# Two attention layers and two gated feed-forward layers: the last chunk's head groups reordered and packed, a norm's reciprocal deviation issued earlier

## The chip, the cores and the metric

The kernel runs on one core of a Trainium2 chip. The metric is the device time of one execution in microseconds (us), lower being better. In the text the engines are PE (TensorE matmul; PEld is its weight load), DVE (VectorE), ACT (ScalarE), POOL (GpSimd) and SP (SyncE, which here only issues DMAs).

## The reference

Four sublayers run one after the other over a residual x of 2048 positions by 448 features, all in float32; the same weights serve both passes.

```
def A(x, wq, wk, wv, wo):             # 16 query heads of 28, one key and value head
    q = (x @ wq) split in 16 heads;  k = x @ wk;  v = x @ wv
    p = softmax(q k^T * 28 ** -0.5)
    return (p @ v, heads joined) @ wo
def B(x, w_gate, w_up, w_down):       # 448 -> 1792 -> 448
    return (silu(x @ w_gate) * (x @ w_up)) @ w_down

x = x + A(layernorm(x));  x = x + B(layernorm(x))
x = x + A(layernorm(x));  x = x + B(layernorm(x))
```

## The kernel before

Positions are cut into four chunks of 512 (`c`), each of four tiles of 128. Matmuls run on float32 numbers split into a high and a low part (`split`, L138 to L140: two POOL instructions), so each product takes three matmuls: high by high, high by low, low by high.

**Scores.** `Attention.scores` works through `GR` (L367), a list of sixteen pairs (chunk, group). A group holds four heads, which sit on 32 partitions each: 28 rows of the head and four spare rows. Each group has sixteen steps (`kt`), one for every 128 keys. A step (L688) runs twelve score matmuls into four PSUM banks (four at a time on 32 rows of the array), and ACT takes the exponential of three banks at once (L704, L710) and of the fourth (L707, L709); on odd steps DVE first copies the fourth bank to SBUF (`raw`, L706). After each odd step the values of the pair of steps before are multiplied in (`pv`, L729) and DVE adds them to the group's accumulator (L746; the first of a group is a copy, L743). One column of the values is 1, so row 28 of each head holds the sum of its exponentials.

**Division.** When a group's last pair is in, `post` (L750) lets SP move the four sum rows to a tile `rs` (L757). Some steps later `rest` runs: five small DVE instructions ending in the reciprocal (L763 to L765), a DMA to DRAM (`rd`, L767), one DMA that broadcasts it to 128 partitions (`rb`, L768, destination 4 x 32 partitions x 512), a multiplication on POOL (L772) and a split into `on` (L773). `rb` and the accumulator `oraw` are halves of one tile (named `o` in the profile).

**Projection by wo.** For the first three chunks the fourth group is dissolved: `spread` (L629) moves the rows of its heads 14 and 15 into the spare rows of the other groups by fourteen small SBUF-to-SBUF DMAs, and copies what is left (two heads, 64 rows) to the upper half. `dense` (L635) then projects two tiles with nine matmuls each on all 128 rows, plus three on each half of the array, which run side by side (`side_by_side`, L353; profile line L358). It runs on PE in the second pair of steps of the next chunk's second group (`between`, L713). The weights `woh` and `wol` are loaded to match (`load_wo(.., True)`). For the last chunk `load_wo(.., False)` loads them again in group 14 without spare rows (memset L612, DMA L619, split on POOL), and `outproj` (L675) uses twelve full matmuls for each of the four tiles.

**Norm.** `norm_steps` (L234) gives the steps of the norm of a projected chunk: four statistics steps (`stat`), `scale` (two POOL instructions, L246 and L247, which make `rstd`), four pairs of `apply` (DVE, L255) and `turn` (DVE transpose, L260), and `send` (four DMAs, L269). The loop at L781 places them for chunks 0 to 2: statistics at steps 4 to 7 of groups 5, 9 and 13, `scale` at step 15, the pairs from step 0 of the next group, `send` at its step 8. In groups 11, 12 and 13, step 8, `weights` (L170) loads feed-forward weights on SP and splits them with twelve POOL instructions (`wgh`, `wgl`, `wdh`, `wdl`).

**End of the attention (L824 to L837).** The first two feed-forward units of chunk 0 (`unit`, L1134; matmuls L338) are laid around the last group's division: unit 0, then `rest` of the last group, then unit 1. Then `outproj` takes three groups for all four tiles, unit 0's second down projection (kept in `ff.left`) runs, and `outproj` takes the last group; DVE adds to the residual `xres`.

Each engine has its own queue and runs it strictly in the order in which the program issues; across engines there are only semaphores.

Of the kernel before, what the change touches and what calls it, by code (L numbers as in the profile page):

```python
# [8 lines left out]
F32 = mybir.dt.float32  # L9
# [43 lines left out]
def forward(  # L53
# [313 lines left out]
    GR = [(c, g) for c in range(NC) for g in range(NG)]  # L367

    class Attention:
# [230 lines left out]
        def scores(self, ff):  # L600
            next(switch)
            with tc.tile_pool(name=f"at{self.layer}", bufs=1, reuse_waits="tile") as wp:
# [6 lines left out]
                def load_wo(z, dense):  # L609
                    r = wpool.tile([P, 4, 2, P], F32, name="wr").rearrange("p (z k) b n -> p z (k b n)", z=2)  # L610
                    if not dense:
                        nc.gpsimd.memset(r, 0.0)  # L612
                    spare = wo[14 * DH : 16 * DH, :].rearrange("(q r) n -> r q n", r=4)
                    for j in range(4):
                        for up in (0, 64) if dense and z and j < 2 else (0,):
                            own = slice(2 * z + bool(up), 2 * z + (1 if dense and z and j > 1 else 2))
                            to = slice(bool(up), own.stop - 2 * z)
                            p0 = up + 32 * j
                            nc.sync.dma_start(r[p0 : p0 + DH, to, 0:D], wos[j][:, own, :])  # L619
                            if dense:  # L620
                                qs = slice(4 * own.start + j, 4 * own.stop - 3 + j, 4)
                                nc.sync.dma_start(r[p0 + DH : p0 + 32, to, 0:D], spare[:, qs, :])
# [6 lines left out]
                def spread(o):  # L629
                    for q in range(14):  # L630
                        p0 = 64 + 4 * q + 4 * (q > 6)
                        dma(o[32 * (q % 4) + DH : 32 * (q % 4) + 32, q // 4], o[p0 : p0 + 4, 3])
                    dma(o[64:128, 3], o[0:64, 3])

                def dense(c, ts, pos, half_first):  # L635
                    o = on[c]
                    cols = [slice(P * t, P * t + P) for t in ts]
                    terms = ((0, woh), (0, wol), (1, woh))

                    def half():  # L640
                        side_by_side(
                            *(
                                [
                                    (po[:, 0:D], (o[rs, 3, v, cs], b[rs, 3, :]), half_first and z == 0, z == 2 and not half_first)
                                    for z, (v, b) in enumerate(terms)
                                ]
                                for cs, po, rs in zip(cols, pos, HALVES)
                            )
                        )

                    def full_tiles(cs, po):
                        for g in range(3):
                            for z, (v, b) in enumerate(terms):
                                nc.tensor.matmul(  # L654
                                    po[:, 0:D], o[:, g, v, cs], b[:, g, :],
                                    start=(g + z == 0 and not half_first), stop=(g + z == 4 and half_first),
                                    skip_group_check=True,
                                )

                    def add(t, po):  # L660
                        x = xres[:, 4 * c + t, :]
                        nc.vector.tensor_tensor(x, po[:, 0:D], x, ALU.add)

                    if half_first:
                        half()
                    for t, cs, po in zip(ts, cols, pos):
                        full_tiles(cs, po)
                        if half_first:
                            add(t, po)
                    if not half_first:  # L670
                        half()
                        for t, po in zip(ts, pos):
# [706 lines left out]
```

## Time and profile before

| what | us |
|---|---|
| median of 3 runs | 1957.73 (1957.02 to 1959.05) |
| the profiled execution, its own time | 1955.75 |
| its span, first to last instruction | 1953.9 |
| PE busy | 1940.9 (99%) |
| ACT busy | 1340.4 (69%) |
| DVE busy | 1020.0 (52%) |
| POOL busy | 790.2 (40%) |

Times in the profile are counted from the start of the span. A row of the timeline holds start, duration, engine, line, operation, output<-inputs, shapes and how many instructions are merged in it; in brackets stands the idle time of the engine just before it, and what ended that. Matmuls overlap, so on PE the distance between starts is what one costs. Layer 0's first accumulate copy (L743) stands at 67.90 us and its last burst ends at 587.72; layer 1's at 1035.80 and 1556.11.

### The profile page before, as it was taken

The numbers are of one execution on the slowest core, as the hardware profiler recorded it, in microseconds if no ns is written. First come the engines' busy times: TensorE is split into PE (matmuls) and PEld (weight loads), VectorE is DVE, ScalarE is ACT, GpSimd is POOL, SyncE is SP. The second block draws the span as 40 slices with busy tenths as digits, with TensorE's granted clock in tenths as the row PEclk, the third lists the DMA queues.
The fourth block names the chain that finished last, engine by engine and source line by source line (L and its number), as shares of the span: only waits on it lengthen the run. The fifth ranks groups of instructions, "written<-read, shape, count | busy, mean of one in ns | idle before, by whom it ended". The sixth has DMA issues, their size and how long they took to land. (4 is left out here: it accounts for less than half of the span.)

```text
span 1953.9 us, 45906 instructions
## 1 busy us (share of the span) xinstructions
PE 1940.9 (99%) x18307; PEld 1303.6 (67%) x18307; DVE 1020.0 (52%) x1711; ACT 1340.4 (69%) x2353; POOL 790.2 (40%) x1021
## 2 busy tenths in 40 slices
PE   9999999999999999999999999999999999999998
PEld 8544444545458889999984445444444688999997
DVE  7443454544435567665654334445545345666653
ACT  4899899898963344444349998989989533444442
POOL 5222111132414868766441221111334167688640
PEclk9999999999999999999999999999999999999999
DMA  5110120021310110010131111202122101110002
GB/s 167 54 32 24 31 56 25 19 76 39 87 35 2 53 33 21 28 32 27 53 114 32 29 29 27 63 23 55 37 64 64 33 11 44 33 32 22 28 17 77
DMA packets 102555, 84.49 MB, mean 43 GB/s; under 512 B 26832, under 2 KB 84816, under 8 KB 102336
## 3 DMA queue, kind: packets, MB, share of 16 engines
q1 hardware_dynamic: 101760, 80.60, 14.8%
q8 instruction: 144, 2.36, 0.5%
q10 hardware_dynamic: 576, 0.92, 0.1%
q14 instruction: 75, 0.61, 0.1%
HBM read 58.99 MB, written 18.74 MB: 40 GB/s over the span
## 5 line engine op out<-in xcount | busy, mean ns | idle before, releaser
L736 PE MATMUL bank<-pt,vsb 128*32 128x512 f32 x4096 | 493.3, 598 | 0.3
L697 PE MATMUL bank<-qstack,keys 32*128 32x512 f32 x1536 | 484.0, 425 | 2.3 <-DVE raw L706 1.4
L697 PE MATMUL three<-qstack,keys 32*128 32x512 f32 x4608 | 461.2, 424 | 1.5 <-DVE vt L573 1.2
L697 PEld LDWEIGHTS three<-qstack,keys 32*128 32x128 f32 x4608 | 254.0, 182 | 294.4 <-ACT pt L710 173.5
L704 ACT ACTIVATE pt<-three 128x1536 f32<-128x1536 f32 x256 | 372.5, 1455 | 1.7 <-PE bank L736 1.3
L710 ACT ACTIVATE pt<-three 128x1536 f32<-128x1536 f32 x256 | 372.1, 1454 | 0.0
L358 PE MATMUL bank<-xh,wgh 64*128 64x512 f32 x1344 | 360.6, 392 | 0.3 <-DVE sg L1176 0.3
L358 PE MATMUL bank<-wdh,h 64*128 64x448 f32 x1776 | 326.5, 364 | 0.1
L706 DVE COPY raw<-bank 128x512 f32<-128x512 f32 x256 | 176.7, 690 | 230.6 <-PE bank L697 227.7
L358 PE MATMUL bank<-xh,wgl 64*128 64x512 f32 x1020 | 289.4, 390 | 0.0
L772 POOL TENSOR_TENSOR o<-o 128x512 f32<-128x512 f32 x32 | 41.2, 1287 | 595.2 <-DMA o<-rd 521.8
L746 DVE TENSOR_TENSOR o<-bank,o 128x512 f32<-128x512 f32 x224 | 154.8, 691 | 230.1 <-PE bank L736 222.6
L736 PEld LDWEIGHTS bank<-pt,vsb 128*32 128x32 f32 x4096 | 107.1, 109 | 250.2 <-issue 153.7
L365 ACT COPY seen<-bank 128x1 f32<-128x1 f32 x788 | 101.0, 164 | 242.9 <-PE bank L358 182.3
L358 PE MATMUL bank<-xl,wgh 64*128 64x512 f32 x912 | 252.0, 390 | 0.0
L697 PEld LDWEIGHTS bank<-qstack,keys 32*128 32x128 f32 x1536 | 243.3, 183 | 4.5 <-DVE raw L706 2.0
L358 PEld LDWEIGHTS bank<-wdh,h 64*128 64x128 f32 x1776 | 233.5, 184 | 10.8 <-issue 2.0
L358 PE MATMUL bank<-wdl,h 64*128 64x448 f32 x888 | 209.7, 366 | 0.0
L358 PEld LDWEIGHTS bank<-xh,wgh 64*128 64x128 f32 x1344 | 197.2, 184 | 13.4 <-issue 1.1
L962 POOL TENSOR_TENSOR xres<-stage,xres 128x448 f32<-128x448 f32 x120 | 151.6, 1275 | 112.9 <-ACT stage L955 112.7
L927 DVE TENSOR_TENSOR xn<-bank,xn 128x512 f32<-128x512 f32 x192 | 126.6, 687 | 125.9 <-PE bank L358 91.4
L709 ACT ACTIVATE pt<-bank 128x512 f32<-128x512 f32 x256 | 151.6, 592 | 54.9 <-PE bank L697 54.8
(214 smaller groups left out, 3066.6 us busy)
## 6 DMA issues: line engine op xcount, KB each, us to landing
o<-rd SPq DMA_DIRECT2D x32, 256.0 KB
qraw<-qd SPq DMA_DIRECT2D x128, 56.0 KB
qd<-stage SPq DMA_DIRECT2D x30, 224.0 KB
xt<-xn SPq DMA_DIRECT2D x28, 224.0 KB
wdr<-in_B_w_down_dram SPq DMA_DIRECT2D x28, 224.0 KB
wr<-in_B_w_gate_dram SPq DMA_DIRECT2D x32, 192.0 KB
wr<-in_B_w_up_dram SPq DMA_DIRECT2D x32, 192.0 KB
xn<-xt SPq DMA_DIRECT2D x6, 768.0 KB
```

Source lines behind the costliest of these rows:

```text
L358: nc.tensor.matmul(po, a, b, start=start, stop=stop, skip_group_check=True)
L365: nc.scalar.copy(seen[:, i : i + 1], po[:, 0:1])
L697: nc.tensor.matmul(three[:, j, :] if j < 3 else one, k[js, kp, ks], q[js, part, :], start=(z == 0), stop=(z == 2), tile_position=(32 * j, 0),)
L704: nc.scalar.activation(pt, three, AF.Exp, scale=SCALE)
L706: nc.vector.tensor_copy(raw, one)
L709: nc.scalar.activation(pt1, one, AF.Exp, scale=SCALE)
L710: nc.scalar.activation(pt, three, AF.Exp, scale=SCALE)
L736: nc.tensor.matmul(po[32 * j : 32 * j + 32, :], vsb[:, n % NT, :], pts[n][j], start=(n == 2 * d), stop=(n > 2 * d), skip_group_check=True,)
L746: nc.vector.tensor_tensor(acc, in_turn(po), acc, ALU.add)
L772: nc.gpsimd.tensor_tensor(rb, oraw, rb, ALU.mult)
L927: plus = lambda out, po, r: tt(by_tile(out), in_turn(po), by_tile(r), ALU.add)
L962: nc.gpsimd.tensor_tensor(r, h[e, t], r, ALU.add)
```

## The change

1. `GR` takes the last chunk's groups in the order 3, 0, 1, 2.
2. For the last chunk's first group (head group 3) the upper 60 rows of the divided result `rb` (heads 14 and 15) are written to DRAM (`two`); `spread` then moves only two pieces (12 and 13) and the copy to the upper half.
3. For its other groups (`ahead`) `post` also sets `rb` to 1.0 on POOL (128x512) and lets SP bring four rows of `two` into the spare rows of each head's accumulator, each DMA behind the DMA that reads that head's sum; `rest` broadcasts to 28 rows of each head by four DMAs in place of one.
4. The second load of `wo` (group 14) is gone, with its memsets and splits; `outproj` is gone, and the last burst uses the packed form, two tiles at a time: the half-row matmuls of a pair of tiles, then two groups for each of the two. The third group of all tiles follows unit 0's second down projection as before.
5. The last group's `rest` is handed to unit 0 as pending work, which puts it behind ACT's cast of `h` and ahead of DVE's low part of `h` (L1180) rather than behind the unit.
6. In the norm steps of chunks 0 to 2 `scale` runs together with the fourth statistics step (step 7), and everything behind it comes three steps earlier (`apply` from step 13, `send` at step 5 of the next group).

The functions `dense` and `outproj` are cut into `half`, `whole` and `add`; for chunks 0 to 2 PE's order does not change by it.

POOL in group 13 of layer 0, before: `wdh`, `wdl` are the last of the weight splits, `qstack` the query split of group 15.

```order
L139 TENSOR_SCALAR wdh<-wdr 128x224
L140 TENSOR_TENSOR wdl<-wdr,wdh 128x224
L246 TENSOR_SCALAR rstd<-mv 128x4
L247 TENSOR_TENSOR rstd<-rstd,halfn 128x4
L139 TENSOR_SCALAR qstack_101<-qraw 128x512
```

The same place now, from the split of the divided group 12:

```order
L139 TENSOR_SCALAR on<-o_5606 128x512
L140 TENSOR_TENSOR on<-o_5606,on 128x512
L246 TENSOR_SCALAR rstd<-mv 128x4
L247 TENSOR_TENSOR rstd<-rstd,halfn 128x4
L139 TENSOR_SCALAR wgh<-wr 128x256
L140 TENSOR_TENSOR wgl<-wr,wgh 128x256
```

The two instructions that make `rstd` have moved from behind the twelve weight splits to ahead of them, right behind the division's.

PE at the start of layer 0's last burst, before (the first row is the end of unit 0's first down projection, `bank_7169` and `bank_7170` are the PSUM banks of tiles 0 and 1):

```order
L358 MATMUL bank_79<-wdh,h_7196 128x448
L680 MATMUL bank_7169<-woh,on 128x448
L680 MATMUL bank_7169<-wol,on 128x448
L680 MATMUL bank_7169<-woh,on 128x448 x2
L680 MATMUL bank_7169<-wol,on 128x448
L680 MATMUL bank_7169<-woh,on 128x448 x2
L680 MATMUL bank_7169<-wol,on 128x448
L680 MATMUL bank_7169<-woh,on 128x448
L680 MATMUL bank_7170<-woh,on 128x448
```

The same place now (`bank_7175` and `bank_7176` are those of tiles 0 and 1; L358 is on half the rows, L651 on all):

```order
L358 MATMUL bank_79<-wdh,h_7202 128x448
L358 MATMUL bank_7175<-woh,on 128x448
L358 MATMUL bank_7176<-woh,on 128x448
L358 MATMUL bank_7175<-wol,on 128x448
L358 MATMUL bank_7176<-wol,on 128x448
L358 MATMUL bank_7175<-woh,on 128x448
L358 MATMUL bank_7176<-woh,on 128x448
L651 MATMUL bank_7175<-woh,on 128x448
L651 MATMUL bank_7175<-wol,on 128x448
L651 MATMUL bank_7175<-woh,on 128x448 x2
L651 MATMUL bank_7175<-wol,on 128x448
L651 MATMUL bank_7175<-woh,on 128x448
```

Nine full matmuls of a tile ahead of the down projection have become three half ones, in pairs with those of the next tile, and six full ones.

SP at the end of layer 0's scores, before and then now (`o_6876` is the last group's accumulator and broadcast, `xd` the next stage's first transfer):

```order
L757 DMA rs<-o_6876 32x1x16 x4
L767 DMA rd<-rs 128x16
L768 DMA o_6876<-rd 128x1x512
L124 DMA xd_7332<-xh 64x512
L124 DMA xd_7333<-xh 64x512
```

```order
L738 DMA rs<-o_6876 32x1x16 x4
L744 DMA o_6876<-two 4x512 x4
L754 DMA rd<-rs 128x16
L757 DMA o_6876<-rd 28x512 x4
L124 DMA xd_7341<-xh 64x512
```

Four small moves stand between the sums and the reciprocal's way to DRAM, and the broadcast is four transfers.

The diff, without the parts that only cut `dense` into pieces:

```diff
-    GR = [(c, g) for c in range(NC) for g in range(NG)]
+    GR = [(c, (g + 3 * (c == NC - 1)) % NG) for c in range(NC) for g in range(NG)]
...
+                row = lambda q: 4 * q + 4 * (q > 6)
+
+                def spread(c):
+                    o = on[c]
+                    for q in range(14) if c < NC - 1 else (12, 13):
+                        dma(o[32 * (q % 4) + DH : 32 * (q % 4) + 32, q // 4], o[64 + row(q) : 68 + row(q), 3])
                     dma(o[64:128, 3], o[0:64, 3])
...
+                def half(c, t, two, start):
+                    side_by_side(
+                        *(
+                            [
+                                (po[:, 0:D], (on[c][rs, 3, v, cs], b[rs, 3, :]), start and z == 0, z == 2 and not start)
+                                for z, (v, b) in enumerate(terms)
+                            ]
+                            for po, cs, rs in zip(two, cols[t : t + 2], HALVES)
+                        )
+                    )
+
+                def whole(c, t, po, gs, start=False, stop=False):
+                    for g in gs:
+                        for z, (v, b) in enumerate(terms):
+                            nc.tensor.matmul(
+                                po[:, 0:D], on[c][:, g, v, cols[t]], b[:, g, :], start=start and g + z == 0,
+                                stop=stop and g + z == 4, skip_group_check=True,
                             )
...
+                    ahead = c == NC - 1 and g < NG - 1
+                    if ahead:
+                        nc.gpsimd.memset(rb, 1.0)
+                        for j in range(4):
+                            p0 = row(4 * g + j)
+                            nc.sync.dma_start(oraw[32 * j + DH : 32 * j + 32, :], on["two"][p0 : p0 + 4, :])
...
-                        nc.sync.dma_start(rb, rd[:, None, :].to_broadcast([4, 32, 512]))
-                        if g == 0:
+                        if ahead:
+                            for j in range(4):
+                                nc.sync.dma_start(rb[32 * j : 32 * j + DH, :], rd[j : j + 1, :].to_broadcast([DH, 512]))
+                        else:
+                            nc.sync.dma_start(rb, rd[:, None, :].to_broadcast([4, 32, 512]))
+                        if i % NG == 0:
                             on[c] = wp.tile([P, NG, 2, 512], F32R, name="on")
...
-                        if g == NG - 1 and c < NC - 1:
-                            spread(o)
-                            todo.append(c)
+                        if c == NC - 1 and g == NG - 1:
+                            on["two"] = dram.tile([60, 512], F32, name="two")
+                            nc.sync.dma_start(on["two"], rb[64:124, :])
+                        if g == NG - 1:
+                            spread(c)
+                            if c < NC - 1:
+                                todo.append(c)
...
+                    fs[3:5] = [lambda fs=fs[3:5]: [f() for f in fs]]
                     for kt, f in enumerate(fs):
-                        later[n + kt + (7 if kt > 3 else 0)] = f
+                        later[n + kt + (5 if kt > 3 else 0)] = f
...
-                    if i == 14 and kt in (2, 12):
-                        later[n + 7], later[n + 8] = load_wo(kt // 8, False)
...
+                ff.pend = [lambda: None, lambda: None, due.popitem()[1]]
                 ff.unit(0, 0, 0)
-                due.popitem()[1]()
                 ff.unit(0, 0, 1)
                 pos = [bank(LOW)[1] for _ in range(4)]
-                for gs in (range(NG - 1), range(NG - 1, NG)):
+                for gs in (range(2), range(2, 3)):
                     for t in range(4):
-                        add = outproj(NC - 1, t, pos[t], gs)
-                        if add:
-                            add()
+                        if 0 in gs and t % 2 == 0:
+                            half(NC - 1, t, pos[t : t + 2], True)
+                        whole(NC - 1, t, pos[t], gs, stop=True)
+                        if 2 in gs:
+                            add(NC - 1, t, pos[t])
                     while ff.left:
                         ff.left.pop(0)()
```

More of the change, by code (lines that the diff above doesn't have):

```diff
@@ L627, in load_wo @@
                     return [lambda: cast(0), lambda: cast(1)]
[L629 to L632, printed above, removed]
-                    dma(o[64:128, 3], o[0:64, 3])
[L635 to L647, printed above, removed]
-                            )
[L649 to L672, printed above, removed]
-                            add(t, po)
```

45 lines of the change are left out of this document (22 added, 23 removed).

## Prediction

> **What bounds the kernel now.** I read the page first, then the table by stage (windows), then the order of time on each engine where two equal stages differ.
>
> ```profile
> PE 1940.9 (99%) x18307; PEld 1303.6 (67%) x18307; DVE 1020.0 (52%) x1711; ACT 1340.4 (69%) x2353; POOL 790.2 (40%) x1021
> ```
>
> PE is busy nearly everywhere, so a saving must shorten what PE does or remove a place where it waits. A "group" below is the sixteen score steps of one entry of GR, numbered 0 to 15 in each layer. In the windows a row holds the stretch and its length, then the busy time of PE, PEld, DVE, ACT, POOL. The first three stretches run from the first accumulate copy (L743) of a group to that of the next, the last one over the burst that ends layer 0's attention.
>
> ```profile
> 215.85:254.41 38.56, 38.56 (x372) 20.13 (x375) 19.81 (x37) 29.62 (x33) 8.22 (x9) 1.00 0.06 15
> 470.78:510.44 39.66, 38.99 (x372) 20.18 (x375) 19.80 (x37) 29.92 (x33) 22.01 (x34) 1.00 0.19 53
> 1438.17:1478.84 40.67, 39.01 (x372) 20.16 (x375) 19.79 (x37) 29.95 (x33) 21.98 (x34) 1.00 0.19 52
> 564.56:587.72 23.16, 23.16 (x118) 19.13 (x118) 5.96 (x13) 3.07 (x9) 3.18 (x3) 1.00 0.23 57
> ```
>
> Group 5 (first row) and group 13 of both layers run the same instructions on PE, DVE and ACT (x372, x37, x33), a projection of the chunk before and its statistics included. Group 13 is 39.66 - 38.56 = **1.10 us** longer in layer 0 and 40.67 - 38.56 = **2.11 us** in layer 1, and PE has holes there that group 5 has not. The difference is POOL's 22 us against 8. In order of time:
>
> ```profile
> 494.96 1.29 POOL L140 TENSOR_TENSOR on<-o,on 128x512 fp32r<-128x512 f32 x1
> ...
> 503.30 0.20 POOL L246 TENSOR_SCALAR rstd<-mv 128x4 f32<-128x4 f32 x1
> 503.58 1.01 POOL L247 TENSOR_TENSOR rstd<-rstd,halfn 128x4 f32<-128x4 f32 x1
> ```
> ```profile
> 504.62 0.80 DVE L255 TENSOR_SCALAR sg<-xres,mv,rstd 128x448 f32<-128x448 f32 x1 [2.06 <-POOL rstd L247]
> 1473.01 0.81 DVE L255 TENSOR_SCALAR sg<-xres,mv,rstd 128x448 f32<-128x448 f32 x1 [3.06 <-POOL rstd L247]
> ```
>
> The norm's rstd stands on POOL behind twelve weight splits, from the division's end to 503.30. DVE waits for it 2.06 and 3.06 us, the raw copy that ACT needs is queued behind that wait, and so a wait of an idle engine becomes time. Price: 2.06 - 1.10 = 0.96 and 3.06 - 2.11 = 0.95 of the wait are absorbed, the rest is lost, one for one.
>
> The burst at the end (last row) has no hole: 23.16 us long, PE 23.16 busy. There only fewer matmuls help, and only if POOL's last group is ready when PE gets to it.
>
> **Term 1: rstd at the last statistics step.** Two POOL instructions move from behind the twelve weight splits to ahead of them; four applies and four transposes on DVE, and the four transfers of the turned chunk on SP, come three steps earlier, in groups 5, 9 and 13 of each layer. Now rstd follows the three POOL steps of the division (L772, L139, L140). In group 13 of layer 0 these ended at 494.96 + 1.29 = 496.25; rstd took 503.30 to 504.59, 1.29; so it would be ready at 497.5. The first apply then stands behind the raw copy of step 13:
>
> ```profile
> 496.31 0.69 DVE L706 COPY raw<-bank 128x512 f32<-128x512 f32 x1 [1.12 <-PE bank L697]
> 498.18 0.69 DVE L746 TENSOR_TENSOR o<-bank,o 128x512 f32<-128x512 f32 x1 [1.18 <-PE bank L736]
> 509.16 1.09 DVE L260 STREAM_TRANSPOSE xn<-sg 128x448 f32<-128x448 f32 x1
> ```
> ```profile
> 1463.38 1.28 POOL L140 TENSOR_TENSOR on<-o,on 128x512 fp32r<-128x512 f32 x1
> 1463.70 0.69 DVE L706 COPY raw<-bank 128x512 f32<-128x512 f32 x1 [1.13 <-PE bank L697]
> 369.36 1.02 POOL L247 TENSOR_TENSOR rstd<-rstd,halfn 128x4 f32<-128x4 f32 x1
> 369.09 0.69 DVE L706 COPY raw<-bank 128x512 f32<-128x512 f32 x1 [1.12 <-PE bank L697]
> ```
>
> DVE is free at 497.0, so the wait left is 0.5 us; in layer 1 rstd would be ready at 1464.66 + 1.29 = 1465.95 against 1464.39, a wait of 1.56. With 0.95 absorbed that costs nothing and 0.6: the cautious end of the term is 1.10 + 1.5 = 2.6 us. But the division itself should end sooner in group 13, since the weight loads that SP issued right behind its broadcast now queue behind the copy of the fourth group to DRAM and two small moves, which wait for POOL. Broadcasts on SP and POOL's start after them:
>
> ```profile
> 486.45 0.57 SPq L768 DMA_DIRECT2D o<-rd  x1
> 492.89 1.29 POOL L772 TENSOR_TENSOR o<-o 128x512 f32<-128x512 f32 x1 [11.19 <-DMA o<-rd]
> 546.78 0.57 SPq L768 DMA_DIRECT2D o<-rd  x1
> 551.96 1.28 POOL L772 TENSOR_TENSOR o<-o 128x512 f32<-128x512 f32 x1 [13.65 <-DMA o<-rd]
> ```
>
> 6.44 us with loads behind it, 5.18 without: 1.26 us sooner, which covers both waits but for 0.3. So I take the whole **3.2 us** (1.10 + 2.11), between 2.6 and 3.2. In groups 5 and 9 nothing is gained. There the closest case is group 9 of layer 0: rstd done at 370.38, DVE free at 369.78, 0.6 late, within what is absorbed. The parity of the steps turns: the apply (0.80 above, beside a busy POOL) now falls into the gap of 1.18 ahead of the accumulate and the transpose (1.09) into the gap of 1.12 ahead of the raw copy. Both fit, the second barely; an overrun of a few tenths is again absorbed, and the cover is the copy's own wait for PE.
>
> What else moves in group 13 costs nothing: the weight loads are issued some 8 us later (an estimate: after POOL's 495, in place of 487), and behind their splits stands the query split of group 15, which is not needed before that group starts. SP's four transfers of the turned chunk now go ahead of a division's sums and broadcast; the accumulator that these hold is needed a group later. The second load of wo, its two memsets and eight POOL casts go; they stood in groups 14 and 15, where POOL idled 13.65 us ahead of a division (551.96), so nothing is gained.
>
> **Term 2: the last burst.** Out go 48 full matmuls, in come 36 full and 12 on half the rows, which run in six pairs. PE, layer 0 (starts, merged rows):
>
> ```profile
> 575.88 0.37 PE L358 MATMUL bank<-wdh,h 64*128 64x448 f32 x2
> 576.18 0.47 PE L680 MATMUL bank<-woh,on 128*128 128x448 f32 x1
> 576.49 0.36 PE L680 MATMUL bank<-wol,on 128*128 128x448 f32 x1
> ...
> 583.37 0.37 PE L680 MATMUL bank<-woh,on 128*128 128x448 f32 x1
> ...
> 585.10 0.47 PE L680 MATMUL bank<-woh,on 128*128 128x448 f32 x1
> ```
>
> From 576.49 to 583.37 stand 34 matmuls: 0.2024 us each, and a pair takes one such slot. 48 slots become 42: 6 x 0.2024 = 1.21 us less. Against it stands each change between full and half rows: 575.88 to 576.18 to 576.49 is 0.61 for two slots, so 0.61 - 0.40 = 0.205 a change. The burst had four (half to full, to half, to full, to half), and has six now: 0.41 more. Net **0.80 us a layer, 1.6 in all**. The Trainium skill, "TensorEngine Tiling (Array Packing)", Key Properties, says that changing the tiling mode drains TensorE; that speaks against this change, and the rows agree with it (0.205 us). Without that rule the term would be 2.4.
>
> PE would reach the last group at 585.10 - 0.80 = 584.3 in layer 0 and, by the rows below, at 1552.7 in layer 1. POOL ended its part at 583.12 + 1.28 = 584.40 and at 1553.09:
>
> ```profile
> 583.12 1.28 POOL L140 TENSOR_TENSOR on<-o,on 128x512 fp32r<-128x512 f32 x1
> 1551.81 1.28 POOL L140 TENSOR_TENSOR on<-o,on 128x512 fp32r<-128x512 f32 x1
> 1553.49 0.47 PE L680 MATMUL bank<-woh,on 128*128 128x448 f32 x1
> ```
>
> So the chain to POOL decides. It starts earlier: the division now stands ahead of h's low part on DVE.
>
> ```profile
> 569.94 0.69 DVE L1176 TENSOR_TENSOR sg<-bank,sg 128x512 f32<-128x512 f32 x1 [4.59 <-PE bank L338]
> 571.98 0.17 DVE L763 TENSOR_SCALAR under<-rs 128x16 f32<-128x16 f32 x1
> 565.38 2.44 SPq L757 DMA_DIRECT2D rs<-o  x4
> 572.97 0.33 SPq L767 DMA_DIRECT2D rd<-rs  x1
> 574.37 0.59 SPq L768 DMA_DIRECT2D o<-rd  x1
> 581.05 1.28 POOL L772 TENSOR_TENSOR o<-o 128x512 f32<-128x512 f32 x1 [25.74 <-DMA o<-rd]
> 212.48 2.38 SPq L443 DMA_DIRECT2D qraw<-qd  x4
> 216.74 0.62 POOL L139 TENSOR_SCALAR qstack<-qraw 128x512 fp32r<-128x512 f32 x1 [15.46 <-DMA qraw<-qd]
> ```
>
> DVE can begin at 570.63 in place of 571.98, 1.35 us sooner. SP has four new moves between rs and rd, each waiting for its own sums: the last sums landed about 1.4 after their issue (as rd did, 572.97 to 574.37), near 568.6, and four issues of 0.59 end near 571.0, ahead of rd at 571.6. The broadcast becomes four transfers of 28 rows. The nearest row is four loads of 28x512: 4.26 us from first issue to POOL. By it POOL starts at 573.0 + 4.3 = 577.3 in place of 581.05, over 3 us ahead of PE. The other end: each costs what the one did (6.68) and the last is issued 1.77 later: 581.5, 0.4 us later than now; PE then waits 0.5 and 0.8 and the term falls to 0.3. I take 1.6. The Trainium skill, "DMA: Bandwidth & Descriptors", Rules for kernel authors, says that an outermost dimension below 16 confines a transfer to that many engines; the old broadcast has 4 outermost, the new ones 28 rows. The 4.26 against 5.18 agrees and lowers the chance of the second rival. The memsets to 1.0 and the noops ahead of the burst cost nothing: POOL idles 25.7 us there.
>
> **Sum.** The profiled execution took 1955.75 us (span 1953.9 and 1.85 around it), 1.98 under the median 1957.73. 1955.75 - 3.2 - 1.6 = 1950.95; on the median **1952.9 us**.
>
> **Rivals.**
> 1. *The wait in group 13 only moves*: weight splits that now run later, beside the applies of group 14, or the transposes in their tight gap, cost what was won. Only term 2 is left: 1957.73 - 1.6 = 1956.1. For it: the gap is 1.12 for 1.09. Against: 0.95 us is absorbed.
> 2. *PE waits for the last group*, as worked out above: 1957.73 - 3.2 - 0.3 = 1954.2. For it: today POOL is only 0.7 and 0.4 us ahead of PE. Against: the chain loses over a microsecond on DVE and gets shorter transfers.
> 3. *Slower*: the apply at step 13 waits at all six places. It stands three steps sooner than now, and rstd right behind a division that waits for a transfer. A rd that lands late does this: in group 13 of layer 1 it took 2.60 to the broadcast, against 1.40 at layer 0's end.
>
> ```profile
> 1452.40 0.36 SPq L767 DMA_DIRECT2D rd<-rs  x1
> 1455.00 0.57 SPq L768 DMA_DIRECT2D o<-rd  x1
> ```
>
>    Groups 5 and 9 are at most 0.6 late, so it decides from 0.35 us more. With 2.4 us late at each of the six places, 6 x 1.45 = 8.7 are lost and 4.8 won: 1961.6. One such rd is seen; six at once are not.
> 4. *More than counted*, if the changes between full and half rows hide behind pairs (0.8) or group 13 gains beyond group 5's length: near 1952.
>
> **Chances.** Forecast 0.55, rival 1 0.15, rival 2 0.14, rival 3 0.06, rival 4 0.10. A measurement of this kernel tells some 0.2%, 3.9 us, from no change: below 1953.8 is faster. The forecast lies only 0.9 under that bound, so I count 0.06 of its 0.55 as no change, and 0.01 of rival 1 as slower: faster 0.59, same 0.34, slower 0.07. The range reaches over rivals 1, 2 and 4 and leaves out the third: 1951.4 to 1956.4.
>
> **What would show it.** In the profile after: the wait of L255 for rstd in group 13 under 1 us, and the stretch between its L743 rows at 38.5 us in both layers (right), or above 39.3 (rival 1). The burst from the first matmul on the first chunk's gate weights to the next chunk's at 22.4 in place of 23.16, with no idle PE ahead of the last group (right); POOL's last split ending after PE arrives (rival 2). Waits of L255 over 1 us in groups 5 and 9: rival 3. Six changes of rows at other than 0.2 us would break term 2.

## The result, and the profile after

The median of ten executions fell from 1957.07 us (ten of the kernel before, 1955.55 to 1960.07) to **1952.31 us** (1951.67 to 1953.48): ratio 0.9975, 95% interval 0.9966 to 0.9985, so 4.8 us less (2.9 to 6.7). The profiled execution took 1952.91 us (span 1951.1), 2.84 less than that of before.

The page's line of engines, and the windows of the changed kernel: group 9 of layer 0, group 13 of both layers, and the two bursts (stretch and length, then the busy time of PE, PEld, DVE, ACT and POOL; the last three numbers are the granted TensorE clock, the busy share of the DMA engines and GB/s).

```profile
PE 1939.6 (99%) x18307; PEld 1298.2 (67%) x18307; DVE 1026.6 (53%) x1711; ACT 1338.5 (69%) x2353; POOL 778.4 (40%) x1007
```
```profile
343.58:382.76 39.18, 38.90 (x372) 20.23 (x375) 22.10 (x40) 29.75 (x33) 8.23 (x9) 1.00 0.06 15
471.39:509.95 38.56, 38.56 (x372) 20.13 (x375) 21.64 (x41) 29.62 (x33) 18.18 (x29) 1.00 0.24 65
1437.44:1476.23 38.79, 38.79 (x372) 20.17 (x375) 21.49 (x40) 29.71 (x33) 16.91 (x27) 1.00 0.24 65
564.10:586.53 22.43, 22.43 (x118) 17.87 (x117) 5.85 (x13) 3.06 (x9) 3.20 (x3) 1.00 0.24 59
1530.39:1552.82 22.43, 22.43 (x119) 17.89 (x118) 5.85 (x13) 3.06 (x9) 3.19 (x3) 1.00 0.23 58
```

Group 13 went from 39.66 to 38.56 us in layer 0 and from 40.67 to 38.79 in layer 1, and PE's holes there closed. Each burst is 0.73 or 0.74 us shorter. Group 9 of layer 0, 38.56 before, now has a hole, a stretch in which PE is idle.

POOL and DVE in group 13 of layer 0 (the first two rows), DVE in layer 1's, and DVE in group 9 of layer 0, in order of time:

```profile
496.01 1.01 POOL L247 TENSOR_TENSOR rstd<-rstd,halfn 128x4 f32<-128x4 f32 x1
497.58 0.51 DVE L255 TENSOR_SCALAR sg<-xres,mv,rstd 128x448 f32<-128x448 f32 x1
...
1464.73 0.51 DVE L255 TENSOR_SCALAR sg<-xres,mv,rstd 128x448 f32<-128x448 f32 x1 [1.08 <-POOL rstd L247]
...
371.25 0.51 DVE L255 TENSOR_SCALAR sg<-xres,mv,rstd 128x448 f32<-128x448 f32 x1 [1.43 <-POOL rstd L247]
371.68 0.68 DVE L727 TENSOR_TENSOR o<-bank,o 128x512 f32<-128x512 f32 x1
372.28 0.98 DVE L260 STREAM_TRANSPOSE xn<-sg 128x448 f32<-128x448 f32 x1
```

Where 2.06 us of waiting stood, DVE no longer waits; in layer 1 the wait fell from 3.06 to 1.08. In group 9 a wait of 1.43 is new; there the accumulate (L727) stands behind the waiting apply, and PE waits for its bank. The transpose now takes 0.98 us.

`rstd` stands behind the division, and the division waits for its reciprocal. In group 9 of layer 0 the kernel before had these rows on SP:

```profile
357.80 0.35 SPq L767 DMA_DIRECT2D rd<-rs  x1
360.19 0.58 SPq L768 DMA_DIRECT2D o<-rd  x1
```

That is 2.39 us from the write to the broadcast, and 2.75 now (357.83 to 360.58). From the broadcast to POOL's start it took 5.44 us and takes 5.88 now. Together that is 0.8 us later.

The end of layer 0's scores: SP's queue, POOL and PE.

```profile
572.56 1.59 SPq L757 DMA_DIRECT2D o<-rd  x4
575.82 1.29 POOL L763 TENSOR_TENSOR o<-o 128x512 f32<-128x512 f32 x1 [22.21 <-DMA o<-rd]
577.90 1.29 POOL L140 TENSOR_TENSOR on<-o,on 128x512 fp32r<-128x512 f32 x1
```
```profile
578.71 0.36 PE L651 MATMUL bank<-woh,on 128*128 128x448 f32 x1
579.00 0.47 PE L358 MATMUL bank<-woh,on 64*128 64x448 f32 x2
579.30 0.36 PE L358 MATMUL bank<-wol,on 64*128 64x448 f32 x2
...
583.86 0.47 PE L651 MATMUL bank<-woh,on 128*128 128x448 f32 x1
```

POOL is done at 579.19, 4.7 us ahead of PE's last group at 583.86 (0.7 before). A change of rows reads as 578.71 to 579.00 to 579.30: 0.59 for two slots of 0.20, so 0.19 for the change.

**What the two traces account for.** From the first accumulate copy to the end of the burst layer 0 took 519.82 us and now 518.51, layer 1 520.31 and now 518.10: 3.5 us. The other stages, whose instructions are the same, took 0.7 more in this one execution. The medians differ by 4.8.

### The profile page after: what moved, and what is told of

Its sections match the earlier page's. It is cut to its first block, busy times and chain, and to the rows that moved or that the text cites. A ratio compares the mean times of both kernels' runs of the same rounds, so it can differ in the third digit from the quotient of the medians.

```text
span 1951.1 us, 45958 instructions
## 1 busy us (share of the span) xinstructions
PE 1939.6 (99%) x18307; PEld 1298.2 (67%) x18307; DVE 1026.6 (53%) x1711; ACT 1338.5 (69%) x2353; POOL 778.4 (40%) x1007
## 5 line engine op out<-in xcount | busy, mean ns | idle before, releaser
L358 PE MATMUL bank<-xh,wgh 64*128 64x512 f32 x1344 | 357.8, 392 | 0.3 <-DVE sg L1172 0.3
L358 PE MATMUL bank<-wdh,h 64*128 64x448 f32 x1776 | 325.7, 364 | 0.1
L358 PE MATMUL bank<-xh,wgl 64*128 64x512 f32 x1020 | 287.7, 390 | 0.0
L727 DVE TENSOR_TENSOR o<-bank,o 128x512 f32<-128x512 f32 x224 | 154.9, 691 | 235.5 <-PE bank L717 227.5
L358 PE MATMUL bank<-xl,wgh 64*128 64x512 f32 x912 | 250.0, 390 | 0.0
L358 PEld LDWEIGHTS bank<-wdh,h 64*128 64x128 f32 x1776 | 228.6, 184 | 11.2 <-issue 2.0
L358 PE MATMUL bank<-wdl,h 64*128 64x448 f32 x888 | 207.9, 366 | 0.0
L358 PEld LDWEIGHTS bank<-xh,wgh 64*128 64x128 f32 x1344 | 193.3, 184 | 14.1 <-issue 1.1
```

The lines of the kernel that those rows point to most:

```text
L358: nc.tensor.matmul(po, a, b, start=start, stop=stop, skip_group_check=True)
L727: nc.vector.tensor_tensor(acc, in_turn(po), acc, ALU.add)
```

## The experiments

"Before" in each comparison is the kernel before, run on the same chip in between. The experiments ran on three chips, where the medians of the kernel before were 1956.74, 1957.09 and 1956.56, so a difference of half a microsecond between the medians of two kernels from different chips can't be told from none. Medians in us:

| run | median | range | ratio to before (95%) |
|---|---|---|---|
| norm edit alone | 1954.78 | 1952.63 to 1958.37 | 0.9990 (0.9981 to 0.9999) |
| packing without the norm edit | 1971.96 | 1971.64 to 1972.85 | 1.0075 (1.0061 to 1.0089) |
| before, weight splits later | 1953.10 | 1952.72 to 1954.31 | 0.9979 (0.9970 to 0.9988) |
| norm edit and later splits | 1954.11 | 1953.01 to 1955.80 | 0.9985 (0.9976 to 0.9994) |
| changed, rstd later at six places | 1968.70 | 1967.24 to 1969.30 | 1.0062 (1.0046 to 1.0077) |
| changed, applies two steps later | 1952.43 | 1951.71 to 1955.52 | 0.9977 (0.9968 to 0.9986) |
| changed, all halves first | 1953.76 | 1952.96 to 1955.76 | 0.9982 (0.9973 to 0.9991) |
| changed, halves joined | 1951.36 | 1950.71 to 1952.70 | 0.9973 (0.9963 to 0.9983) |
| halves joined, later splits in place of the norm edit | 1951.29 | 1950.58 to 1952.08 | 0.9973 (0.9961 to 0.9984) |

### The norm edit alone

```diff
+                    fs[3:5] = [lambda fs=fs[3:5]: [f() for f in fs]]
                     for kt, f in enumerate(fs):
-                        later[n + kt + (7 if kt > 3 else 0)] = f
+                        later[n + kt + (5 if kt > 3 else 0)] = f
```

> The kernel before with edit 6 alone (rstd at the last statistics step, everything behind it three steps earlier); groups in the old order, the second load of wo and the unpacked burst stay. Theory (the two terms add, and the first is the wait of group 13): 2.6 to 3.2 us less than before, 1953.9 to 1954.5 us; stretch of group 13 at 38.6 us in layer 0 and 38.6 to 39.2 in layer 1, since here the broadcast keeps its 6.44 us; burst still 23.16. The ten times should lie as close together as those of the changed kernel (1.8 us) and not as wide as those of before (4.5), if it is that wait which differs from one execution to the next. Rival (the wait only moves, and the packing won the 4.8): 1957 us, with waits of L255 elsewhere.

Measured 1954.78, 2.0 us less, short of the 2.6 to 3.2 expected. Group 13 of layer 0 is cured; in layer 1 a wait is left:

```profile
470.80:509.29 38.49, 38.49 (x372) 20.20 (x375) 21.86 (x41) 29.61 (x33) 22.05 (x34) 1.00 0.20 54
1437.17:1476.21 39.04, 38.88 (x372) 20.19 (x375) 21.99 (x41) 29.71 (x33) 22.30 (x34) 1.00 0.19 53
```
```profile
1453.75 0.58 SPq L768 DMA_DIRECT2D o<-rd  x1
1459.85 1.28 POOL L772 TENSOR_TENSOR o<-o 128x512 f32<-128x512 f32 x1 [11.29 <-DVE raw L706]
1464.62 0.59 DVE L255 TENSOR_SCALAR sg<-xres,mv,rstd 128x448 f32<-128x448 f32 x1 [1.24 <-POOL rstd L247]
```

The broadcast still takes 6.10 us to POOL's start, and the apply at step 13 waits 1.24. Group 9 of layer 0 has a wait of 1.03 and took 38.77 us. The theory's size holds for group 13 of layer 0; the times are not closer together than before, so that part of it failed.

### The packing without the norm edit

The changed kernel with the three lines above reversed.

> The changed kernel without edit 6: scale back at step 15, behind the weight splits. Theory (a wait for rstd is lost one for one but for 0.95 us): the splits now end near 511.4 and 1479.0 us, since their loads queue behind the copies of the fourth group; rstd would be ready near 512.7 and 1480.3, DVE asks for it at 502.6 and 1470.0, so 10.1 and 10.4 us of wait, 9.2 and 9.4 lost against 1.1 and 2.1 before. With 1.5 won in the two bursts that is 13.9 us more than before: 1971 us; group 13 near 47.8 us in both layers. Rival (the two parts are independent): 1.5 us less than before, 1955.6 us.

Measured 1971.96, 15.2 us more than before, and no other group changed. Windows of group 13 of both layers, then DVE and PE in layer 0:

```profile
470.35:519.03 48.68, 41.05 (x372) 21.04 (x375) 19.71 (x37) 29.95 (x33) 21.60 (x34) 0.89 0.19 52
1446.28:1495.61 49.33, 40.67 (x372) 20.97 (x375) 19.74 (x37) 29.93 (x33) 21.58 (x34) 0.90 0.19 52
```
```profile
511.62 0.81 DVE L255 TENSOR_SCALAR sg<-xres,mv,rstd 128x448 f32<-128x448 f32 x1 [9.47 <-POOL rstd L247]
513.08 0.79 PE L669 MATMUL bank<-qstack,keys 32*128 32x512 f32 x1 [7.63 <-DVE raw L678]
```

The theory's mechanism holds: packing pushes the weight loads behind the copies of the fourth group, the splits behind the loads, and rstd behind the splits. But 10.2 us are lost in layer 0 (48.68 - 38.5) with a wait of 9.47, so nothing was absorbed. The window's clock of 0.89 points to the reason; it is taken up below.

### Later weight splits in place of the norm edit

```diff
-                    if kt == 8 and 10 < i <= 11 + FG:
-                        ff.W[i - 11] = weights(i - 11)
+                    if kt == 8 and 10 < i < 11 + FG or (i, kt) == (14, 0):
+                        ff.W[min(i - 11, FG)] = weights(min(i - 11, FG))
```

> The kernel before, with the third set of feed-forward weights loaded and split from step 0 of group 14 rather than step 8 of group 13; nothing else changes, scale stays at step 15. Theory (the twelve weight splits ahead of rstd are the whole of group 13's excess): group 13 takes 38.6 us in both layers, 3.2 us less in all: 1953.9 us, with times as close together as in the changed kernel. Rival (the excess belongs to the division's late broadcast and its three POOL steps): group 13 still 39.7 and 40.7 us, 1957 us.

Measured 1953.10, 3.6 us less. Group 13, where scale was not touched, gives 3.3 of it:

```profile
471.04:509.56 38.52, 38.52 (x372) 20.14 (x375) 20.28 (x37) 29.61 (x33) 21.73 (x34) 1.00 0.21 54
1437.22:1475.70 38.48, 38.48 (x372) 20.15 (x375) 20.25 (x37) 29.59 (x33) 21.72 (x34) 1.00 0.21 54
```

The twelve splits are the whole excess of group 13, and the theory holds to 0.1 us in the windows: 1.10 and 2.11 forecast, 39.66 - 38.52 = 1.14 and 40.67 - 38.48 = 2.19 measured. The broadcast stayed late here, 6.10 and 6.40 us to POOL's start, so the rival is out.

### Both cures together

The two edits above on the kernel before.

> The kernel before with both the norm edit and the later weight splits (third set from step 0 of group 14). Theory (both take the same wait away, so they don't add): about 1953.1 us as with the later splits alone, group 13 at 38.5 us in both layers. The norm edit alone gave 1954.8 with times from 1952.6 to 1958.4; if the loads and splits in group 13 are what spreads them, they lie within 2 us here; if it is the early apply, they stay 4 us and more apart. Rival (two gains that add): 1951 us.

Measured 1954.11: they don't add. But the theory's 38.5 us in both layers did not come. The early apply still waits, 1.77 us in group 13 of layer 1 (39.47 us) and 1.23 in group 9 of layer 0 (38.99 us), and the times lie 2.8 us apart, between the two cases named. In group 13 the broadcast took 6.16 and 6.56 us to POOL's start, with loads still issued behind it: the query's, then the weights' of group 14. By these waits the later place of scale is the safer one when the splits are out of the way. The medians of the two kernels, 1953.10 and 1954.11, don't show it, since the intervals of their ratios overlap.

### rstd later at all six places

The two instructions run three times over (`times=3`):

```diff
...
-            nc.gpsimd.tensor_scalar(rstd, mv[:, 4 * c + m * z : 4 * c + m * z + m, 1], 1.0, EPS, ALU.mult, ALU.add)
-            nc.gpsimd.tensor_tensor(rstd, rstd, halfn[:, 0:m], ALU.pow)
+            for _ in range(times):
+                nc.gpsimd.tensor_scalar(rstd, mv[:, 4 * c + m * z : 4 * c + m * z + m, 1], 1.0, EPS, ALU.mult, ALU.add)
+                nc.gpsimd.tensor_tensor(rstd, rstd, halfn[:, 0:m], ALU.pow)
...
```

> The changed kernel with the two POOL instructions of scale run three times over for chunks 0 to 2 (the same result each time), so that rstd comes 2 x 1.29 = 2.6 us later at all six places. In the changed kernel's trace rstd is 0.0, 1.4 and -0.6 us late for DVE in groups 5, 9 and 13 of layer 0, and 0.0, 0.0 and 1.05 in layer 1. Theory (a wait is lost one for one but for some 0.83 us, as group 9's 1.43 gave 0.62 and group 13's 1.08 gave 0.24): waits of 2.6, 4.0, 2.0, 2.6, 2.6 and 3.6, lost 17.4 - 5.0 = 12.4 in place of 0.9, so 11.5 us more than the changed kernel: 1963.8 us. Rival (the earlier place leaves slack that the trace doesn't show): under 5 us more.

Measured 1968.70, 16.4 us more than the changed kernel, for 11.5 expected. Group 9 of layer 0, then groups 5 and 13 of layer 1 (the third number from the right is the granted clock), and a finer cut of the first of them, around the end of PE's hole:

```profile
345.43:388.55 43.12, 40.49 (x372) 20.53 (x375) 22.19 (x41) 29.88 (x33) 10.64 (x13) 0.96 0.06 14
1190.45:1232.59 42.14, 40.55 (x372) 20.61 (x375) 22.01 (x40) 29.91 (x33) 10.64 (x13) 0.96 0.06 15
1450.39:1491.10 40.71, 38.87 (x372) 20.17 (x375) 21.36 (x41) 29.72 (x33) 21.85 (x35) 1.00 0.23 62
```
```profile
376.00:378.00 2.00, 1.37 (x13) 0.64 (x17) 1.78 (x3) 0.00 (x0) 0.55 (x1) 0.93 0.00 0
378.00:380.00 2.00, 2.00 (x16) 0.43 (x8) 1.67 (x2) 0.60 (x1) 1.34 (x2) 0.50 0.00 0
380.00:382.00 2.00, 2.00 (x24) 0.87 (x20) 0.86 (x2) 1.37 (x2) 0.00 (x0) 0.72 0.00 0
```

DVE and PE in the same three groups (L256 is the apply here, L728 the accumulate, L670 a score matmul):

```profile
375.46 0.51 DVE L256 TENSOR_SCALAR sg<-xres,mv,rstd 128x448 f32<-128x448 f32 x1 [3.79 <-POOL rstd L248]
376.63 0.49 PE L670 MATMUL bank<-qstack,keys 32*128 32x512 f32 x1 [2.63 <-DVE o L728]
...
1219.47 0.51 DVE L256 TENSOR_SCALAR sg<-xres,mv,rstd 128x448 f32<-128x448 f32 x1 [2.74 <-POOL rstd L248]
1220.64 0.66 PE L670 MATMUL bank<-qstack,keys 32*128 32x512 f32 x1 [1.59 <-DVE o L728]
...
1479.58 0.51 DVE L256 TENSOR_SCALAR sg<-xres,mv,rstd 128x448 f32<-128x448 f32 x1 [2.98 <-POOL rstd L248]
1480.75 0.50 PE L670 MATMUL bank<-qstack,keys 32*128 32x512 f32 x1 [1.84 <-DVE o L728]
```

The clock is 1.00 in four of the six groups, and there the law holds: in the last row, 2.98 waited, 40.71 - 38.5 = 2.2 lost, 0.8 absorbed. In the two with 0.96 more is lost than was waited: 43.12 - 38.5 = 4.6 for 3.79, and 3.6 for 2.74. There the granted clock fell to 0.50 after PE's hole, for 3.4 us. That is the part that the theory lacked, about 1.6 us each time. The six windows together are 14.7 us longer than in the changed kernel; without twice 1.6 that is the 11.5 expected. The profiled execution was the fastest of the four (1967.24), 14.3 us over that of the changed kernel. What the slower ones lost beyond it can't be seen.

The Trainium skill, "TensorE: Matmul & The Clock Gate", Part 1, says that an idle window of about 3.4 us puts the array on half its clock, and that the window is free-running. The half clock agrees (0.50). Its limit doesn't: holes of 1.59 and 2.63 us were enough here. That 1.84 us did not do it fits a window that runs on its own.

The clock records of the traces bear out such a window. Both drops here last 3.413 us, and they begin 843.09 us apart (at 377.72 and 1220.81), which is 247 times 3.413. In the kernel with the packing alone both last three times 3.413, and they begin 286 times that apart. Cut into these steps, the hole of 1.59 us lies whole in one step, at whose end the clock fell, and that of 2.63 has 2.32 in one. The hole of 1.84 falls into 1.32 and 0.52. Behind no step with 1.32 us of idle PE or less does the clock fall in any of the traces, so the limit lies here between 1.32 and 1.59 us of idle PE in one step.

### The applies two steps later

`5 if kt > 3` becomes `7 if kt > 3` in the changed kernel.

> The changed kernel with the applies and all behind them two steps later (first apply at step 15, on odd steps as in the changed kernel; scale still at step 7). Theory (rstd is sometimes late at step 13, by an amount that differs from one execution to the next): 0.6 and 0.24 us of groups 9 and 13 come back, 38.5 us in all six groups: 1951.5 us, and the times lie closer together than 1.8 us. Rival (those waits are the profiled execution's alone): 1952.3 us, as wide as before.

Measured 1952.43, with times as far apart as 1951.71 and 1955.52. All six groups took 38.46 to 38.62 us in its trace, so the slack is there; yet the median did not move, and the times are wider than the changed kernel's 1.8 us. The rival holds for the loss: three other packed kernels with the apply at step 13 (all halves first, halves joined, last division behind unit 0; see below) wait 0.70, 0.68 and 0.41 us in group 9 of layer 0 in their traces and lose nothing there. The wait itself is in all of them, and 1.43 is the largest.

### Two ways to four changes of rows

All half-row pairs first:

```diff
+                for t in (0, 2):
+                    half(NC - 1, t, pos[t : t + 2], True)
                 for gs in (range(2), range(2, 3)):
                     for t in range(4):
-                        if 0 in gs and t % 2 == 0:
-                            half(NC - 1, t, pos[t : t + 2], True)
```

> The changed kernel with both pairs of half-row matmuls of the last burst ahead of all full ones: four changes between half and full rows in the burst in place of six, the same number of matmuls. Theory (each change costs 0.2 us of PE): the burst takes 22.03 us in place of 22.43 in each layer, 0.8 us less in all: 1951.5 us. Rival (what stands beside a change is the cost of a pair of half-row matmuls, not of the change): 22.43 as before, 1952.3 us.

Measured 1953.76, 1.4 us above the changed kernel. The burst in layer 0, longer by 0.87 us, and PE in its second pair:

```profile
564.98:588.28 23.30, 22.78 (x118) 18.11 (x117) 5.85 (x13) 3.06 (x9) 3.18 (x3) 1.00 0.22 57
```
```profile
577.57 0.47 PE L358 MATMUL bank<-woh,on 64*128 64x448 f32 x1 [0.27 <-ACT sg L1171]
578.30 0.47 PE L358 MATMUL bank<-woh,on 64*128 64x448 f32 x1 [0.25 <-DVE sg L1172]
```

Neither theory named this. The banks of tiles 2 and 3 were unit 1's gate and up banks. ACT and DVE still read them, and PE waited for both. So the run says nothing about the price of a change. The second way asks for no bank sooner; it puts the pair of tiles 2 and 3 beside the down projection:

```diff
...
+                    if 0 in gs:
+                        half(NC - 1, 0, pos[0:2], True)
                     for t in range(4):
-                        if 0 in gs and t % 2 == 0:
-                            half(NC - 1, t, pos[t : t + 2], True)
-                        whole(NC - 1, t, pos[t], gs, stop=True)
+                        whole(NC - 1, t, pos[t], gs, start=t > 1, stop=True)
...
+                    if 0 in gs:
+                        half(NC - 1, 2, pos[2:4], False)
```

> The changed kernel with the half-row matmuls of tiles 2 and 3 in the last burst moved behind those tiles' full ones, next to unit 0's second down projection, which is on half rows too: four changes between half and full rows in place of six. In the run with all half rows first the second pair waited for banks that unit 1 still held (23.30 us). Here no bank is asked for sooner than in the changed kernel. Theory (a change costs 0.2 us, and that run lost by the banks alone): burst 22.03 us in place of 22.43, 1951.5 us. Rival (fewer changes bring nothing): 22.43, 1952.3 us.

Measured 1951.36. The bursts:

```profile
563.24:585.23 21.99, 21.99 (x118) 18.04 (x117) 5.83 (x13) 3.05 (x9) 3.19 (x3) 1.00 0.23 60
1528.65:1550.66 22.01, 22.01 (x117) 18.05 (x117) 5.83 (x13) 3.05 (x9) 3.19 (x3) 1.00 0.24 60
```

22.43 - 22.00 = 0.43 us for two changes, 0.215 each: the same matmuls in another order. The theory holds.

The same kernel, with the three lines of the norm edit reversed and the later weight splits put in as above:

> The changed kernel with the joined halves (four changes of rows), the norm back at step 15 and the third set of weights from step 0 of group 14. Theory (what cost 19 us in the run without the norm edit was only that the splits stood ahead of rstd): the same as with the joined halves and the norm edit, 1951.4 us, group 13 at 38.5 and the burst at 22.0 us. Rival (the late loads behind the fourth group's copy delay group 13 whatever stands behind them): 1955 us or more.

Measured 1951.29, group 13 at 38.46 us in both layers and the burst at 21.99. The theory holds, and between the two cures no difference shows in the packed kernel. These two kernels have the lowest medians of all, about a microsecond under the changed one. Against the kernel before on their own chips the ratios are 0.9973 for 0.9975, which the intervals don't tell apart: what is shown is the burst, 0.43 us shorter in each layer.

### The chain to POOL

The kernel before with the last broadcast in four pieces of 32 rows:

```diff
+                        for j in range(4) if i == len(GR) - 1 else ():
+                            nc.sync.dma_start(rb[32 * j : 32 * j + 32, :], rd[j : j + 1, :].to_broadcast([32, 512]))
+                        if i < len(GR) - 1:
+                            nc.sync.dma_start(rb, rd[:, None, :].to_broadcast([4, 32, 512]))
-                        nc.sync.dma_start(rb, rd[:, None, :].to_broadcast([4, 32, 512]))
```

> The kernel before, with the last group's one broadcast of the reciprocal cut into four of 32 rows each; nothing else. Theory (a broadcast in pieces of many rows lands sooner): POOL starts its multiplication 3.3 to 4.3 us after the first issue in place of 6.7, its last split ends near 581 and 1550 us instead of 584.4 and 1553.1; the burst is still 23.16 us, since PE didn't wait. Rival (the four transfers take as long as the one, and the changed kernel's lead of 4.7 us came from elsewhere): 6.7 us and more.

```profile
574.42 1.73 SPq L769 DMA_DIRECT2D o<-rd  x4
577.96 1.30 POOL L775 TENSOR_TENSOR o<-o 128x512 f32<-128x512 f32 x1 [22.52 <-DVE sg L1179]
580.05 1.30 POOL L140 TENSOR_TENSOR on<-o,on 128x512 fp32r<-128x512 f32 x1
```

3.54 us in place of 6.68 (4.19 in layer 1), POOL done at 581.35; the burst stayed at 23.18 and the one time was 1955.41. So four pieces land sooner than one transfer, also without packing. This agrees with the rule of "DMA: Bandwidth & Descriptors" in the Trainium skill that the prediction weighed.

The changed kernel with the last division behind unit 0 again:

```diff
-                ff.pend = [lambda: None, lambda: None, due.popitem()[1]]
+                ff.pend = [lambda: None, lambda: None]
                 ff.unit(0, 0, 0)
+                due.popitem()[1]()
```

> The changed kernel with edit 5 undone: the last group's division stands behind unit 0 on DVE again, behind h's low part. Theory (DVE's order is 1.35 us of the lead that POOL won, the four transfers the rest): POOL starts near 577.2 us counted as in the changed kernel's trace, 4.8 us after the last sums' reciprocal could be had in place of 3.4; its last split is still 3.3 us ahead of PE, and the burst stays 22.43 us. Rival (POOL's start falls back behind PE's arrival): the burst grows by the wait.

```profile
577.32 1.29 POOL L763 TENSOR_TENSOR o<-o 128x512 f32<-128x512 f32 x1 [23.62 <-DMA o<-rd]
579.40 1.28 POOL L140 TENSOR_TENSOR on<-o,on 128x512 fp32r<-128x512 f32 x1
583.98 0.47 PE L651 MATMUL bank<-woh,on 128*128 128x448 f32 x1
```

POOL is done at 580.68, 3.3 us ahead of PE, the burst at 22.41, the one time 1952.51. Edit 5 is worth 1.4 us of lead (4.7 against 3.3) and nothing in the burst.

### The norm edit alone, once more

The same kernel as in the first experiment.

> The norm edit alone once more, since its times ran from 1952.6 (the profiled one) to 1958.4 us. Theory (the apply at step 13 has no slack, and a reciprocal that lands late differs between executions): if this execution takes 1954 us or more, the excess over the first stands in groups 5, 9 or 13, with waits of L255 for rstd. Rival (the spread belongs to other stages): the six groups as in the first, the excess ahead of the scores or in the feed-forward parts.

It took 1955.71, 3.08 us more than the first profiled execution of the same kernel. The first accumulate copy of the first execution; that of the second, its apply in group 13 of layer 1, and the window of that group:

```profile
67.91 0.69 DVE L743 COPY o<-bank 128x512 f32<-128x512 f32 x1 [0.81 <-PE bank L736]
```
```profile
69.74 0.69 DVE L743 COPY o<-bank 128x512 f32<-128x512 f32 x1 [0.81 <-PE bank L736]
...
1467.40 0.59 DVE L255 TENSOR_SCALAR sg<-xres,mv,rstd 128x448 f32<-128x448 f32 x1 [2.21 <-POOL rstd L247]
```
```profile
1438.89:1478.97 40.08, 38.95 (x372) 20.18 (x375) 22.01 (x40) 29.74 (x33) 22.29 (x34) 1.00 0.19 52
```

Both theories have a share: 1.83 us of the excess stand ahead of the scores, where all kernels here run the same instructions, and 1.04 in group 13 of layer 1. The first share may belong to the chip: this execution ran on another chip than the first, and all four traces from there begin the scores at 69.0 to 70.1 us, all four from another chip at 67.9 to 68.1.

## Why the prediction was right, point by point

The forecast was 1952.9 us (4.8 less than the median then known), and 1952.31 (4.8 less than the median of ten) came. That the two agree to a tenth is luck: the terms measured 2.4 and 1.5 us in the windows, for 3.2 and 1.6 in the sum, and where the rest of the median's 4.8 lies is not shown. The steps did not all hold as well as the sum.

- **Group 13's excess is the wait behind the weight splits: shown.** Taking only the splits away gave the whole of it, and putting the splits further back cost 15 us.
- **The size of term 1, 3.2 us.** 1.10 + 1.88 = 2.98 came back in group 13, and 0.62 was lost again in group 9 of layer 0: 2.4 in the profiled execution, under the 2.6 to 3.2 forecast. The step "in groups 5 and 9 ... within what is absorbed" was off there: 0.6 late by the rows of before, to which 0.36 came in the reciprocal's way to the broadcast and 0.44 in the broadcast, and the wait became 1.43. It is the mechanism of rival 3, at one place of six. The prediction said that one late reciprocal is seen; the rows of before have a second at that very place, 2.39 us, and the trace of every run has late ones at the same two of the six places (2.1 to 2.8 us). In the traces of the packed kernels with all halves first and with joined halves, which keep the norm edit, groups 5, 9 and 13 took 38.47 to 38.59 us, so there the whole term is had.
- **The price, "one for one" with 0.95 absorbed.** It held where the clock stayed at 1.00, for waits up to 2.98 us, with 0.6 to 0.8 absorbed in the later runs. It fails once PE's hole lowers the clock, which a wait of 2.74 already did.
- **The division ends sooner in group 13, and covers layer 1's wait but for 0.3: right in the main, and needed.** The broadcast took 5.15 and 5.57 us, 5.18 forecast. In layer 1 a wait of 1.08 us was left, where the prediction had 0.3 and looked for under 1, and 0.3 us was lost. The norm edit alone, with loads still behind the broadcast, took 6.10 and 6.59 in layer 1 and lost 0.5 and 1.6 us there. So the "cautious end" describes the norm edit without the packing, and the two parts of the change lean on each other: alone they gave 2.0 us less and 15.2 more.
- **The weight loads, "some 8 us later": at no cost, but only because rstd had left.** The first was issued at 499.24 in place of 487.07, 12 us later; the splits began 8 us later. The prediction looked for what stands behind them and found a query split; with scale there it is the largest wait of this study.
- **The gap of the transposes** was tight by the rows of before (1.09 for 1.12); now they took 0.98. Rival 1 cost nothing: group 14, beside the splits that run later, took 29.62 and 29.60 us, for 29.56 and 29.55 before.
- **Term 2, 0.80 us a layer:** 0.73 and 0.74. A change costs 0.215 by the joined halves, for 0.205 by the rows.
- **The chain to POOL:** 575.82 against 577.3 forecast; the four pieces took 3.26 us where the nearest row had 4.26, and the reciprocal was sent at 571.10 for 571.6. Rival 2 was 4.7 us away.

**What stays open.** The traces account for 3.5 us of the 4.8; the interval (2.9 to 6.7) covers both, and what the untraced executions did can't be seen. Of single executions, the stretch ahead of the first accumulate copy alone differed from 67.6 to 70.1 us over all the traces, as much as the larger term gave. Why it differs was not tried. Why the norm edit alone had times up to 1958.4 is settled only in part.

## What to carry to other kernels

Before a wait on an in-order queue is moved, look at everything that will stand ahead of it in the new place and at whose transfers come late there: the same twelve splits cost 3.3 us, nothing or 21 us in the windows of group 13, according to whether rstd stood behind them and how late their loads came. A change in the order of loads can make another part of the same change necessary, so try each part alone. When matmuls are put in another order, ask which banks they need sooner, and place those on part of the rows beside others of their kind.

## What the runs showed of the hardware

- The granted clock fell to 0.50 for one step of 3.413 us behind a step with 1.59 us of idle PE, and not behind one with 1.32; the steps run on their own, so a hole of 1.84 us that fell into two did nothing. Such a drop cost about 1.6 us beside the wait.
- In layer 0's last division a broadcast from DRAM to 128 partitions in one transfer of 4 x 32 rows took 6.68 us to its user, in four transfers of 28 or 32 rows 3.26 and 3.54 (6.94, 3.23 and 4.19 in layer 1), although SP then needs 1.6 to 2.4 us to issue them.
- Over all the traces a broadcast with other loads issued right behind it took 5.8 to 6.6 us in group 13, without them 4.9 to 5.6.
